# One core, LSH attention into a mixture of experts: the bucket projection reads the q and k that the scores already hold, loads move behind the exchange, v gets a third buffer, and routing and scatters move to earlier places

## The chip, the cores and the metric

The kernel runs on one core of one Trainium2 chip. The metric is the device time of one execution in microseconds (us), less is better. The engines are TensorE (PE; its weight loads are listed apart as PEld), VectorE (DVE), ScalarE (ACT), GpSimd (POOL) and SyncE (SP), which here only issues transfers. Each engine works through its own instructions in order and waits on semaphores for the others.

## The reference

Attention in which a query sees only the keys of its own bucket, then a mixture of experts with one expert per token, all in float32:

```python
q, k, v: [4, 8, 768, 64];  proj: [64, 6]
q_bits = (einsum('bhsd,dk->bhsk', q, proj) > 0)      # and the same for k
q_bucket = sum(q_bits * 2**arange(6))                # and the same for k
mask = q_bucket[:, :, :, None] == k_bucket[:, :, None, :]
scores = where(mask, (q @ k.T) / 8, -1e9)
attn = exp(scores - max);  attn = attn / (attn.sum(-1) + 1e-9)
x = (attn @ v) as [3072, 512]                        # token, 8 heads x 64
logits = x @ w_gate                                  # [512, 8]
e = argmax(logits);  gate = softmax(logits)[e]
y = gate * (relu(x @ w1[e]) @ w2[e])                 # w1 [8,512,1024], w2 [8,1024,512]
```

## The kernel before, in words

The 32 heads are worked through two at a time. I call the two heads of one step a **pair**; there are 16, numbered 0 to 15, four per batch. The outer loop is `for g in range(NG)`. What every engine does inside a pair, and in which order, is a table of words written out by hand: `HEAD` for pair 0, `NEXT` for pair 1, `PLAN` for pairs 2 to 14, `LAST` for pair 15. `step` turns a word into instructions; a word with a `-` belongs to the pair before.

The words that matter here:

- `S0` to `S11` (`score`, L302 and L304): the 12 score tiles of a pair, 128 queries by 768 keys, for its two heads in turn. The scores land in three PSUM buffers named `s`.
- `R` (`peak`, L312): VectorE's row maximum of a tile. `A` (`factor`, L317 to L321): bias and scale from it, on GpSimd where the word ends in P. `X` (`expo`, L328): ScalarE's exponential, which frees the PSUM buffer.
- `T`, `E`: half of the probability tiles are transposed on TensorE (L342) and copied out. `D` (`turn`, L382): the other half is transposed in 32x32 blocks by VectorE into the tile `w2`, and `Y` (`exchange`, L391) moves the blocks to their partitions by 16 transfers SBUF to SBUF into `pt`. It is issued at the start of the next pair.
- `B` and `V` (`pv`, L402): probabilities times v (tile `vt`). `K`, `L` (`tok`, L421, and `tok_ev`, L431): the result per token, with the gate's logits beside it.
- `G` (`lsh_mm`, L260): the projection of q and k of the next pair on the six random directions. `H` (`lsh_ev`, L243): the signs, on ScalarE. `w` (`lsh_bits`): GpSimd scales half of them and SP writes them to DRAM (`masks<-bits`, L271). `z0`, `z1` (`mask`, L275): GpSimd issues two transfers that read them back, one per head, into 16 rows of the next pair's operands (`qk` or `w`). With these rows the score product itself puts the masked scores out of reach, so `S0` and `S1` of the next pair cannot start before `z0` and `z1` have landed.
- `Z` (`route_step`): the routing of a batch (argmax of the logits, a running count per expert, the slot of each token), once per batch, in pairs 5, 9 and 13. `N` (`scatter_step`): the scatter of 128 token rows to their slots in DRAM (L496), issued by GpSimd.
- `C` (`part`): GpSimd splits the next pair's q and k into high and low parts.

The loads are called from `before(c)` when `score` starts an even tile: `load_x` (q and k of one head, `xd`, or `w` for odd pairs, 768 KB), `load_pair` (the same q and k of two heads once more, packed on 128 partitions, `xhe`, 768 KB, read by `lsh_mm` alone), `load_v` (`vt`, 384 KB) and `fill` (`sorted_rows<-xr`, 1156 KB of empty rows into the slots, eight times in all). All of them, the exchange and the write of the bits go through SP's one queue in the order of the program: what waits there holds up what stands behind it.

After pair 15 the eight experts follow, as matrix products over sorted tokens. The change leaves them as they are.

## Time and profile before

| what | value |
|---|---|
| median of 3 runs | 798.16 us (795.27 to 802.81) |
| the profiled execution | 803.59 us, of which 801.8 us lie between its first and last instruction |
| attention, pairs 1 to 14 | 35.1 to 446.5 us of the span |
| TensorE busy | 739.3 us (92%) |
| GpSimd busy | 513.0 us (64%) |
| data moved | 148.13 MB, mean 185 GB/s |

The experts fill the span's last 320 us with TensorE nearly always busy; what there is of idle time on TensorE lies in the attention. A pair is measured here from its first row maximum on VectorE (L312) to the next pair's. All times of the trace are microseconds from the first instruction of that one execution.

### The profile page before, as it was taken

Reading aid. Unit: us, or ns where it says so; the run is one execution under the profiler, and the core shown is the slowest. Engines: PE = TensorE matmul, PEld = TensorE weight load, DVE = VectorE, ACT = ScalarE, POOL = GpSimd, SP = SyncE. Lnnn points to the kernel's source line nnn. Section 1 sums busy time; section 2 is a strip of 40 time slices with the busy share of each in tenths; the row PEclk is TensorE's granted clock in tenths of the full one; section 3 lists DMA queues with packets and bytes.
Section 4 is the critical chain, followed back from the end, with each engine's and each line's share of the span. In section 5 each row is a group of like instructions: output and inputs, shape, how many; then the busy total and the mean of one; then the engine's idle time right before and its main releaser. Section 6 shows DMA issues by size and latency. Waiting matters only on the chain.

```text
span 801.8 us, 12935 instructions
## 1 busy us (share of the span) xinstructions
PE 739.3 (92%) x4315; PEld 585.6 (73%) x4315; DVE 458.7 (57%) x861; ACT 403.7 (50%) x800; POOL 513.0 (64%) x800
## 2 busy tenths in 40 slices
PE   8987979778979898899989899999999999999996
PEld 4765657355666566567656678989999999989895
DVE  7666868476758777788867856322272723232221
ACT  6765666363656565577646662443444443434320
POOL 6845757465857676787868555566465757667532
PEclk8998999899989999999988999999999999999999
DMA  7549699797896869779765843845435458545301
GB/s 262 193 153 227 192 267 250 217 248 228 236 250 155 230 172 225 225 217 247 189 178 146 212 138 138 282 131 200 165 129 183 128 147 173 164 144 190 115 9 36
DMA packets 59124, 148.13 MB, mean 185 GB/s; under 512 B 12451, under 2 KB 16291, under 8 KB 59056
## 3 DMA queue, kind: packets, MB, share of 16 engines
q1 hardware_dynamic: 52224, 130.92, 57.3%
q0 software_dynamic: 6688, 16.35, 6.2%
q8 instruction: 35, 0.57, 0.3%
q14 instruction: 33, 0.27, 0.1%
q10 hardware_dynamic: 144, 0.02, 0.0%
HBM read 88.39 MB, written 26.33 MB: 143 GB/s over the span
## 4 chain that ended last, share of the span: by engine, by line
PE 62%; DMA 14%; POOL 6%; issue 6%; DVE 5%; ACT 3%; SPq 3%; POOLq 0%; another core or an unknown queue 0%; DVEq 0%; ACTq 0%
PE s L746 16%; PE s L783 9%; PE t L402 9%; PE s L803 7%; PE s L302 6%; PE s L304 5%; PE t L342 4%; DMA qk<-masks 4%; DMA pt<-w 3%; DMA w<-masks 3%; DVE m L312 3%; PE t L421 2%; ACT e L328 2%; SPq L391 2%; DMA masks<-bits 2%
## 5 line engine op out<-in xcount | busy, mean ns | idle before, releaser
L328 ACT ACTIVATE e<-s,m 128x768 f32<-128x768 f32 x192 | 190.1, 991 | 141.4 <-POOL m L321 122.3
L312 DVE TENSOR_REDUCE m<-s 128x1 f32<-128x768 f32 x192 | 180.1, 950 | 61.6 <-PE s L304 54.2
L674 POOL TENSOR_TENSOR w<-raw,w 128x512 fp32r<-128x512 f32 x112 | 142.4, 1302 | 45.7 <-ACT w L673 45.5
L402 PE MATMUL t<-pt,vt 128*64 128x384 f32 x768 | 135.8, 504 | 16.8 <-DMA pt<-w 10.8
L746 PE MATMUL s<-xh,w 128*128 128x456 f32 (+6 forms) x672 | 126.8, 346 | 0.0
L746 PEld LDWEIGHTS s<-xh,w 128*128 128x128 f32 x672 | 119.1, 188 | 2.9
L402 PEld LDWEIGHTS t<-pt,vt 128*64 128x64 f32 x768 | 54.4, 141 | 83.9 <-issue 76.5
L342 PE MATMUL t<-ident,e 128*128 128x128 f32 x648 | 92.8, 279 | 11.2 <-ACT pt L368 7.8
L342 PEld LDWEIGHTS t<-ident,e 128*128 128x128 f32 x648 | 74.3, 141 | 26.9 <-ACT pt L368 13.1
L382 DVE STREAM_TRANSPOSE w<-e 128x768 f32<-128x768 f32 x84 | 78.5, 959 | 23.4 <-DMA pt<-w 9.1
L762 DVE SCALAR_TENSOR_TENSOR hh<-s,hh 128x256 fp32r<-128x256 f32 (+7 forms) x64 | 35.5, 555 | 91.4 <-ACT hh L760 90.0
L783 PE MATMUL s<-hh,w 128*128 128x456 f32 (+3 forms) x384 | 78.7, 359 | 0.0
L317 POOL TENSOR_SCALAR m<-m 128x1 f32<-128x1 f32 x126 | 29.4, 233 | 74.2 <-DVE m L312 70.2
L302 PE MATMUL s<-qk 80*128 80x384 f32 x192 | 60.7, 401 | 12.7 <-DMA qk<-masks 12.5
L783 PEld LDWEIGHTS s<-hh,w 128*128 128x128 f32 x384 | 69.9, 188 | 2.4
L368 ACT ACTIVATE pt<-t 128x512 f32<-128x512 f32 (+1 forms) x113 | 65.2, 588 | 12.3 <-PE t L342 11.8
L302 PE MATMUL s<-w 80*128 80x384 f32 x192 | 58.7, 387 | 13.1 <-DMA w<-masks 9.6
L760 ACT ACTIVATE hh<-s 128x256 fp32r<-128x256 f32 (+7 forms) x64 | 31.3, 489 | 75.9 <-PE s L746 75.9
L816 POOL DMA_INDIRECT out_dram<-y,ix x26 | 26.0, 999 | 67.6 <-DVE y L814 31.7
L673 ACT ACTIVATE w<-raw 128x512 fp32r<-128x512 f32 x112 | 66.4, 623 | 2.5 <-DMA raw<-in_w_dram 2.4
L803 PE MATMUL s<-w,hh 128*128 128x512 f32 (+1 forms) x240 | 58.9, 398 | 0.0
L304 PE MATMUL s<-qk 128*128 128x384 f32 x192 | 53.8, 363 | 0.7 <-DVE qk L228 0.7
(209 smaller groups left out, 1076.7 us busy)
## 6 DMA issues: line engine op xcount, KB each, us to landing
raw<-in_w_dram SPq DMA_DIRECT2D x64, 512.0 KB, 3.7
pt<-w SPq DMA_DIRECT2D x224, 144.0 KB, 4.3
xd<-in_qk_dram SPq DMA_DIRECT2D x16, 768.0 KB, 5.5
xhe<-in_qk_dram SPq DMA_DIRECT2D x15, 768.0 KB, 7.1
w<-in_qk_dram SPq DMA_DIRECT2D x14, 768.0 KB, 5.7
sorted_rows<-xr SPq DMA_DIRECT2D x8, 1156.0 KB
xg<-sorted_rows SPq DMA_DIRECT2D x25, 289.0 KB, 4.9
vt<-in_v_dram SPq DMA_DIRECT2D x16, 384.0 KB, 3.5
```

Of the source, the lines that this page charges most:

```text
L302: nc.tensor.matmul(p[:, a, :HALF], k[0:80, 2, c], k[0:80, 3, n], start=i >= 4, stop=i < 4)
L304: nc.tensor.matmul(p[:, a, :HALF], k[:, 0, c], k[:, 1, n], start=i < 4, stop=i >= 4)
L312: nc.vector.tensor_reduce(m[:, 0:1], p[:, :, :HALF], axis=AX.XY, op=OP.max, negate=True)
L328: nc.scalar.activation(e, p[:, :, :HALF], AF.Exp, bias=m[:, 2:3], scale=m[:, 1:2], accum_out=SM[g, hf][:, t, s:s + 1])
L342: nc.tensor.transpose(p[:, x * 128:(x + 1) * 128], e[w][:, kt // 3, (kt % 3) * 128:(kt % 3) * 128 + 128], ident)
L382: nc.vector.transpose(d.rearrange("p b k q -> p k b q"), PP.pop(i).rearrange("p a c -> p (a c)"))
L402: nc.tensor.matmul(p[s * 64:(s + 1) * 64, :HALF], VT[g][:, kt, s, :], x, start=(kt == 0), stop=(kt == NT - 1))
L673: nc.scalar.activation(w[:, 0, a], r, AF.Copy)
L674: nc.gpsimd.tensor_tensor(w[:, 1, a], r, w[:, 0, a], op=OP.subtract)
L746: nc.tensor.matmul(p[:, :c], w[:, a, d, fs], x[:, b, d, :c], start=(k == 0), stop=(k == 11))
L783: nc.tensor.matmul(p[:, :c], w[:, a, f % 4, ms], h[b][:, f, :c], start=(k == 0), stop=(k == 23))
L803: nc.tensor.matmul(p[:pw], HH[n][b][:, f, i:i + pw], w[:, a, f % 4], start=(k == 0), stop=(k == 23))
```

## The change

It has five parts. (1) `lsh_mm` no longer reads `xhe` but the tiles `xd` that the scores use. Those hold each head's q and k twice, on partitions 0 to 63 and 64 to 127, so the projection is now 16 products instead of 4: 64 rows deep, 192 columns wide, two heads (`s`) added up in PSUM, the two halves of the columns (`r`) on the two halves of the rows, into two PSUM buffers `t` instead of one. `lsh_ev` takes two sign instructions of 192 columns instead of one of 384. `load_pair` and its 15 loads go. (2) `load_x` of both heads moves from the words `S0` and `S4` to `S6`, so behind the exchange in SP's queue. (3) `vt` has three buffers instead of two. (4) The fills move from pairs 1 to 4 to pairs 0 to 3. (5) In `PLAN` the routing words `Z` move to the front of the pair, and the six scatters of a batch are spread: in batches 0 and 1 two in each of three pairs (words `N3` and `N4`, then `N0` and `N3` twice), where it was one, three and two; in batch 2 two and four, where it was one and five. `N4` stands between `z0` and `z1`; it was used in the first and the second of these pairs (5 and 6, 9 and 10, 13 and 14), and is now used in the first alone.

```diff
@@ -51,7 +51,7 @@
 
 
 @with_exitstack
-def lsh_attention_moe(ctx, tc, qk, qk2, v, proj, wg, w1, w2, out):
+def lsh_attention_moe(ctx, tc, qk2, v, proj, wg, w1, w2, out):
     nc = tc.nc
     const = ctx.enter_context(tc.tile_pool(name="const", bufs=1))
     moe = ctx.enter_context(tc.tile_pool(name="moe", bufs=1))
@@ -64,7 +64,7 @@
     tabd = nc.dram_tensor("spill_rows", [TMAX, 128, 2], I32).ap()
 
 
-    XD, XL, VT = {}, {}, {}
+    XD, VT = {}, {}
 
 
     room = moe.tile([128, 2, 2 * S], F32, name="w3")
@@ -76,17 +76,12 @@
             nc.sync.dma_start(x[:, c[0]:c[1]], qk2[h][:, c[0]:c[1]])
         XD[h] = x
 
-    def load_pair(g):
-        x = moe.tile([128, 2 * S], F32, name="xhe")
-        nc.sync.dma_start(x, qk[2 * g:2 * g + 2].rearrange("s d c -> (s d) c"))
-        XL[g] = x
-
     def load_v(g):
-        VT[g] = wk.tile([128, NT, 2, D], F32, name="vt")
+        VT[g] = wk.tile([128, NT, 2, D], F32, name="vt", bufs=3)
         nc.sync.dma_start(VT[g], v[g])
 
     load_x(0)
-    pj = const.tile([128, 32], F32, name="pj")
+    pj = const.tile([128, 64], F32, name="pj")
     nc.scalar.dma_start(pj, proj)
     load_x(1)
     small = const.tile([128, 1], F32, name="small")
@@ -235,7 +230,7 @@
 
         p = LP[-h, k] = ps.tile([128, 512], F32, name="t", bufs=2)
         for a in (2 * k, 2 * k + 1):
-            nc.tensor.matmul(p[32 * a:32 * a + 32, :HALF], pj[0:64], XD[h][0:64, a * HALF:(a + 1) * HALF],
+            nc.tensor.matmul(p[32 * a:32 * a + 32, :HALF], pj[0:64, 0:32], XD[h][0:64, a * HALF:(a + 1) * HALF],
                              start=True, stop=True)
 
     def signs(o, i, at=0):
@@ -254,15 +249,21 @@
 
     def lsh_mm(g):
 
-        x = XL.pop(g)
-        p = ps.tile([128, 512], F32, name="t", bufs=2)
-        for a in range(4):
-            nc.tensor.matmul(p[32 * a:32 * a + 32, :HALF], pj, x[:, a * HALF:(a + 1) * HALF], start=True, stop=True)
-        LP[g] = p
+        LP[g] = p = [ps.tile([128, 512], F32, name="t", bufs=2) for _ in range(2)]
+        n = HALF // 2
+        for s in range(2):
+            for a in range(4):
+                for r in range(2):
+                    d = slice(64 * r, 64 * r + 64)
+                    nc.tensor.matmul(p[r][32 * a:32 * a + 32, :n], pj[d, 32 * s:32 * s + 32],
+                                     XD[2 * g + s][d, a * HALF + r * n:a * HALF + r * n + n],
+                                     start=(s == 0), stop=(s == 1))
 
     def lsh_ev(g):
         BT[g] = wk.tile([128, HALF], F32, name="bits", bufs=1)
-        signs(BT[g], LP.pop(g)[:, :HALF])
+        n = HALF // 2
+        for r, p in enumerate(LP.pop(g)):
+            signs(BT[g][:, r * n:r * n + n], p[:, :n])
 
     def lsh_bits(g):
 
@@ -846,7 +847,6 @@
 
 
     late_consts()
-    load_pair(1)
     load_x(2)
     load_x(3)
     load_v(0)
@@ -890,7 +890,7 @@
 
     HEAD = """
         k01A k00V j00V j01P y01 q00A p00V y00 q01P l00V b03 p01P f0 b00 b02 l01P b01 k10A f1 k11A y11 j10P p10A R0
-        q10A S1 j11P b12 y10 R1 l10P b13 S2 X0 G b10 p11P s01 R2 X1 b11 S3 q11P H S4 X2 w R3 T00 T01 E00a l11P S5 R4
+        q10A S1 j11P b12 y10 R1 l10P b13 S2 X0 b10 p11P s01 R2 X1 b11 G S3 q11P H S4 X2 w R3 T00 T01 E00a l11P S5 R4
         E01a T02 X3 s00 R5 E02a s02 T10 X4 S6 E10v X5 R6 T11 S7 s10 E11a T12 s13 R7 E12a T20 X6 S8 s03 E20v T21 X7
         S9 z0 E21v T22 s11 R8 T30 E22a S10 s14 E30a s15 T31 X8 R9 V0 M0 X9 E31v R10 s12 z1 s05 T32 O0 s04 S11 E32a
         T40 X10 R11 K0
@@ -904,10 +904,10 @@
     """.split()
 
     PLAN = """
-        O0- S0 S1 Y0- C00 C01 C02 K0- S2 R0 R1 A0P A1P L0- G C03 C04 R2 X0 Z0 A2V S3 R3 Z1 X1 N0 S4 H A3P X2 R4 T00
-        E00a T01 S5 N1 X3 Z2 E01v T02 T10 R5 S6 A4P C05 E02v A5P R6 X4 E10a T11 X5 T12 A6V w M1- E11a S7 N2 C06 C10 S8
-        C11 R7 X6 A7V T20 E12a S9 E20v N3 R8 C12 T21 X7 R9 A8P C13 E21a C14 A9P T22 X8 z0 S10 D6 B10- E22a Z3 Z4 R10
-        Z5 Z6 D7 X9 A10P X10 N4 S11 R11 B11- B00 z1 D8 O1- A11P B01 D9 X11 C15 K1- D10 C16 D11 M0 L1-
+        O0- S0 S1 Y0- C00 C01 C02 K0- Z0 S2 R0 R1 Z1 A0P A1P L0- G C03 C04 R2 X0 Z2 A2V S3 R3 X1 N0 S4 H Z3 A3P X2 Z4
+        R4 Z5 T00 E00a T01 S5 N1 X3 E01v T02 T10 R5 Z6 S6 A4P C05 E02v A5P R6 X4 E10a T11 X5 T12 A6V w M1- E11a S7 N2
+        C06 C10 S8 C11 R7 X6 A7V T20 E12a S9 E20v N3 R8 C12 T21 X7 R9 A8P C13 E21a C14 A9P T22 X8 z0 S10 D6 B10- E22a
+        R10 D7 X9 A10P X10 N4 S11 R11 B11- B00 z1 D8 O1- A11P B01 D9 X11 C15 K1- D10 C16 D11 M0 L1-
     """.split()
 
     LAST = """
@@ -932,21 +932,21 @@
 
         b, q = divmod(g - NP, NP)
         if 0 <= b < B - 1:
-            at = {(1, 4): 0, (2, 0): 1, (2, 1): 2, (2, 2): 3, (2, 3): 4, (2, 4): 5} if b == B - 2 else                 {(1, 4): 0, (2, 0): 1, (2, 2): 2, (2, 4): 3, (3, 0): 4, (3, 2): 5}
+            late = {(2, 1): 3, (2, 2): 4, (2, 3): 5} if b == B - 2 else {(2, 3): 3, (3, 0): 4, (3, 3): 5}
+            at = {(1, 3): 0, (1, 4): 1, (2, 0): 2} | late
             if (q, k) in at:
                 scatter(b, at[q, k] // 3, (at[q, k] % 3,))
 
     def before(c):
 
         g, r = divmod(c, 6)
-        if g + 2 < NG and r in (0, 2) and g + 2 != NG - 1:
-            load_x(2 * g + 4 + r // 2)
+        if r == 3 and g + 2 < NG - 1:
+            load_x(2 * g + 4)
+            load_x(2 * g + 5)
         if g + 1 < NG and r == 4:
             load_v(g + 1)
-        if g + 2 < NG and r == 3:
-            load_pair(g + 2)
-        if 0 < g < 5 and r > 3:
-            fill((g - 1) * 2 + r - 4)
+        if g < 4 and r > 3:
+            fill(2 * g + r - 4)
 
     def behind(i):
 
@@ -1169,13 +1169,13 @@
     q, k, v = (np.asarray(inputs[n]) for n in "qkv")
     qk = np.ascontiguousarray(np.stack([q, k], 2).transpose(0, 1, 4, 2, 3)).reshape(B * H, D, 2 * S)
     vv = np.ascontiguousarray(v.reshape(B, NP, 2, NT, 128, D).transpose(0, 1, 4, 3, 2, 5)).reshape(NG, 128, NT, 2, D)
-    pj = np.zeros((2, D, 32), np.float32)
+    pj = np.zeros((2, D, 64), np.float32)
     wg = np.zeros((2, D, NP, 2 * E), np.float32)
     for s in range(2):
-        pj[s, :, s * 16:s * 16 + 12] = np.tile(inputs["proj"], 2)
+        pj[:, :, s * 48:s * 48 + 12] = np.tile(inputs["proj"], 2)
         wg[s, :, :, s * E:s * E + E] = np.asarray(inputs["moe_w_gate"]).reshape(NP, 2, D, E)[:, s].transpose(1, 0, 2)
-    pj, wg = pj.reshape(2 * D, 32), wg.reshape(2 * D, NP, 2 * E)
-    arrays = {"in_qk_dram": qk, "in_qk2_dram": np.concatenate([qk, qk], 1), "in_v_dram": vv, "in_proj_dram": pj, "in_wg_dram": wg,
+    pj, wg = pj.reshape(2 * D, 64), wg.reshape(2 * D, NP, 2 * E)
+    arrays = {"in_qk2_dram": np.concatenate([qk, qk], 1), "in_v_dram": vv, "in_proj_dram": pj, "in_wg_dram": wg,
               "in_w1_dram": np.ascontiguousarray(inputs["moe_w1"]), "in_w2_dram": np.ascontiguousarray(inputs["moe_w2"])}
     nc = bacc.Bacc("TRN2", target_bir_lowering=False, num_devices=1, dynamic_dma_scratch_size=2048)
     args = [nc.dram_tensor(n, a.shape, mybir.dt.from_np(a.dtype), kind="ExternalInput").ap() for n, a in arrays.items()]
```

SP's queue around the pairs 3 and 4, where the fills are still going. The names: `masks<-bits` is the write of the bits, `sorted_rows<-xr` two fills, `pt<-w_...` the 16 transfers of one exchange. Before:

```order
L271 DMA masks<-bits 128x384
L86 DMA vt<-in_v_dram 128x768
L149 DMA sorted_rows<-xr 512x1x578 x2
L76 DMA xd<-in_qk_dram 128x1536
L391 DMA pt<-w_1295 32x1152 x16
L76 DMA xd<-in_qk_dram 128x1536
L81 DMA xhe<-in_qk_dram 128x1536
L271 DMA masks<-bits 128x384
```

And after:

```order
L272 DMA masks<-bits 128x384
L81 DMA vt<-in_v_dram 128x768
L144 DMA sorted_rows<-xr 512x1x578 x2
L392 DMA pt<-w_1343 32x1152 x16
L76 DMA xd<-in_qk_dram 128x1536 x2
L272 DMA masks<-bits 128x384
```

The load of q and k ahead of the exchange has gone behind it, in the place of `xhe`; two loads of 768 KB still stand ahead of the write of the bits.

VectorE at the start of pair 5, where batch 0 is routed: `xr<-t,r` is the word `L`, `m<-s` a row maximum, `rl<-xr` and `rf<-rl` are the routing's reductions. Before:

```order
L431 TENSOR_TENSOR xr<-t,r 128x3x144
L312 TENSOR_REDUCE m<-s 128x1 x2
L431 TENSOR_TENSOR xr<-t,r 128x3x144
L312 TENSOR_REDUCE m<-s 128x1
L453 TENSOR_REDUCE rl<-xr 128x24 x2
L454 TENSOR_REDUCE rf<-rl 128x6
```

And after:

```order
L432 TENSOR_TENSOR xr<-t,r 128x3x144
L454 TENSOR_REDUCE rl<-xr 128x24 x2
L455 TENSOR_REDUCE rf<-rl 128x6
L313 TENSOR_REDUCE m<-s 128x1 x2
L460 TENSOR_REDUCE rf<-rl 128x6
L432 TENSOR_TENSOR xr<-t,r 128x3x144
```

The first reductions of the routing now stand ahead of the pair's first two row maxima, and its next one ahead of the `xr<-t,r` for which the projection waits.

## Rows read from the trace of the kernel before

**Rows 1.** SP's own waits, whole run: who for whom, us in total, times, longest

```profile
SPq L86 <- PE t L402: 120.3, 13, 10.5
```

**Rows 2.** Busy us (count) by engine in stretches; then granted clock, DMA share, GB/s

```profile
252.60:277.10 24.50, 24.08 (x152) 16.49 (x151) 20.97 (x34) 16.64 (x33) 18.15 (x35) 1.00 0.85 225
388.10:414.10 26.00, 24.88 (x159) 16.68 (x158) 22.44 (x43) 17.04 (x34) 18.83 (x40) 1.00 0.66 179
277.10:307.00 29.90, 26.46 (x159) 18.62 (x159) 22.74 (x43) 17.27 (x34) 20.67 (x44) 0.94 0.69 188
128.10:161.00 32.90, 26.62 (x154) 17.95 (x153) 20.93 (x34) 16.75 (x33) 18.36 (x35) 0.90 0.86 238
35.10:446.50 411.40, 361.60 (x2165) 250.50 (x2164) 298.88 (x501) 239.46 (x471) 283.07 (x547) 0.95 0.78 214
```

**Rows 3.** Waits of the engines, whole run: us in total, times, longest

```profile
PE s L302 <- DMA qk<-masks: 12.5, 4, 5.3
...
PE t L402 <- DMA pt<-w: 10.8, 3, 5.2
...
PE s L302 <- DMA w<-masks: 9.6, 3, 4.8
...
PE t L402 <- DMA xd<-in_qk_dram: 5.9, 1, 5.9
```

**Rows 4.** Timeline of TensorE: first instruction after four of these waits

```profile
69.39 0.98 PE L302 MATMUL s<-qk 80*128 80x384 f32 x2 [5.34 <-DMA qk<-masks]
...
147.88 0.91 PE L402 MATMUL t<-pt,vt 128*64 128x384 f32 x2 [5.91 <-DMA xd<-in_qk_dram]
...
279.19 0.91 PE L302 MATMUL s<-w 80*128 80x384 f32 x2 [2.14 <-DMA w<-masks]
...
461.95 1.51 PE L402 MATMUL t<-pt,vt 128*64 128x384 f32 x8 [1.39 <-DMA pt<-w]
```

**Rows 5.** Timeline of SP's issues, pairs 1, 4 and 8: start, us, what

```profile
53.03 1.31 SPq L149 DMA_DIRECT2D sorted_rows<-xr  x2
...
122.98 1.29 SPq L149 DMA_DIRECT2D sorted_rows<-xr  x2
...
125.96 17.41 SPq L391 DMA_DIRECT2D pt<-w  x16
...
263.60 0.38 SPq L271 DMA_DIRECT2D masks<-bits  x1
271.58 0.33 SPq L86 DMA_DIRECT2D vt<-in_v_dram  x1
272.00 0.38 SPq L76 DMA_DIRECT2D w<-in_qk_dram  x1
275.58 10.78 SPq L391 DMA_DIRECT2D pt<-w  x16
```

**Rows 6.** Mask reads issued at 60.30, 270.94 and 272.01: KB, us to landing

```profile
qk<-masks POOLq DMA_DIRECT2D x1, 96.0 KB, 9.0
...
w<-masks POOLq DMA_DIRECT2D x1, 96.0 KB, 2.7
...
w<-masks POOLq DMA_DIRECT2D x1, 96.0 KB, 7.0
```

**Rows 7.** Groups by line and form: busy us, mean ns of one, idle before

```profile
L260 PE MATMUL t<-xhe,pj 128*32 128x384 f32 x120 | 14.8, 568 | 0.0
...
L243 ACT ACTIVATE bits<-t,small 128x384 f32<-128x384 f32 x15 | 8.6, 576 | 6.3 <-PE t L260 6.3
...
L453 DVE TENSOR_REDUCE rl<-xr 128x24 f32<-128x192 f32 x8 | 3.9, 510 | 0.1
```

**Rows 8.** The routing's tile `rl`: ns min/median/max of one instruction on GpSimd

```profile
L461 POOL TENSOR_SCALAR oh<-rl x3: 326/326/329, 167.1 to 394.2; 128x48 bf16<-128x48 f32 x3
```

**Rows 9.** Timeline of ScalarE and TensorE at the start of pair 13

```profile
389.77 0.99 ACT L328 ACTIVATE e<-s,m 128x768 f32<-128x768 f32 x1 [2.79 <-POOL m L321]
...
390.15 0.85 PE L260 MATMUL t<-xhe,pj 128*32 128x384 f32 x8
390.94 0.62 PE L302 MATMUL s<-w 80*128 80x384 f32 x2
```

## What I predict

> **What bounds the kernel now.** I read the stretches first. Pair 8 takes 24.5 us, and TensorE is busy for 24.08 of them at a granted clock of 1.00 [rows 2]: an undisturbed pair is bound by TensorE, and the others hide behind it. Pairs 1 to 14 together take 411.4 us with TensorE busy for 361.6 and a mean clock of 0.95, so about 50 us are idle, and pairs such as 4 (32.9 us, clock 0.90) and 9 (29.9 us, clock 0.94) are well above 24.5 [rows 2]. The waits say for what: seven for a mask (12.5 and 9.6 us), three for the exchange (10.8), and one of 5.9 put down to a load of q and k [rows 3]. The timeline shows this last one at a product with v, whose other operand comes by the exchange [rows 4]; I count it with the exchange. That is 38.8 us in eleven waits, and each is a transfer that landed late.
>
> Why they land late is in SP's queue and in the landings. The load of v cannot be issued before the second product with v of the pair before has read its buffer; SP stood for this 120.3 us in all [rows 1]. It is let go at the pair's end, at 271.58 in pair 8, with the load of q and k right behind it at 272.00 [rows 5]. The first mask read went out at 270.94, ahead of both, and landed in 2.7 us; the second at 272.01, behind them, took 7.0 [rows 6], and TensorE stood for 2.14 us at its first use [rows 4]. So a read on GpSimd's queue does not overtake what SP's queue holds. For the fills it is the same: in pair 1 two were issued at 53.03 [rows 5], and the mask read of 60.30 took 9.0 us [rows 6] and cost 5.34 [rows 4]. In pairs 2 to 4 the fills wait behind the load of v until the pair's end, and stand, with a load of q and k, right ahead of the exchange: 122.98, then 125.96 with 17.41 us for the 16 issues, where those at the start of pair 9 took 10.78 [rows 5]. That is the wait of 5.91 at 147.88 [rows 4], and two more like it.
>
> **What goes.** With three buffers the load of v needs a product that ended a whole pair earlier, so it follows the write of the bits at once, some 8 us ahead of the mask reads (in pair 8 the write is at 263.60 [rows 5]). The load of q and k stands behind the exchange, in the slot of the packed copy that goes; both had the same size, so the write of the bits keeps what it has ahead of it. From pair 5 on nothing of SP is then issued right ahead of the mask reads, and the exchange, at 275.58, comes after them. I take off all 38.8 us but the exchange wait of the last pair, 1.39 at 461.95 [rows 4], where the queue stays as it was: 37.4. After each wait TensorE runs for a while at the lower of its two clock levels (1.2 and 2.4 GHz); 0.05 of 411.4 us [rows 2] is 20.6 us of full clock that was not granted, of which I take a little over half as lost on work, 12 (the rest fell into the idle time itself). Together 49. The lengths agree: pair 9 is 5.4 us over pair 8 for a wait of 2.14, pair 4 is 8.4 over for one of 5.91.
>
> **What is put in its place.** *Fills.* They are now issued behind the write of the bits in pairs 0 to 3, where those of pair 1 stood already. So the exchange is free of them, but the mask reads of pairs 1, 2 and 3 find them ahead. In pair 1 the 5.34 us had a load of q and k in the queue too, which is gone; I take 2 us each, and 1.3 for the clock: 10 us. Bounds: nothing, if the bits are ready early, and three times 5.34 with 2.5 of clock, 23. Pair 0 has until pair 1 to read its masks; I take nothing there, 3 at most.
>
> *Routing early.* In pairs 5, 9 and 13 two reductions of 0.51 us [rows 7] and a small one stand ahead of the first row maximum. Then GpSimd does five operations of about 0.33 [rows 8] ahead of the first factor, which the first exponential waits for (389.77 in pair 13); TensorE began the fourth score tile at 390.94 [rows 9], as soon as that exponential freed a buffer. The first exponential moves back by 1.0 at least and by 2.8 if all of it queues up. Pair 13 pays for the old place too: it takes 26.0 us against 24.5 for pair 8 [rows 2]. Net 1.5 a pair, so 4.5 us; bounds 0 and 8.
>
> *The projection.* Eight passes take 0.85 us on TensorE [rows 9], though one takes 568 ns on average [rows 7]: the four column quarters run side by side. Now 32 passes of half the width run on eight tiles of the array. If the two row halves also overlap, the streaming time is what it was, plus a start for twice as many rounds; if they don't, it doubles, 0.85 more. No row of this trace shows two row halves at once, and a gain has no source, since no fewer columns are streamed. I take 0.2, nearer to the overlap that the quarters show. The second sign instruction costs at most half of the 576 ns [rows 7] again, on ScalarE, which stands between two exponentials there; I take 0.1 of it as seen. So 0.3 for 15 pairs, 4.5 us; bounds 0 and 15 times 1.1, 17. The second PSUM buffer is the one that `xr<-t,r` frees; the projection waited for that before, so this is free, except in the routing pairs, where it is counted above.
>
> The page TensorEngine Tiling of the Trainium skill (Tiling Modes) lists eight tiles of 64 rows by 32 columns and says that tiles work independently; by that the term is the low one, and no run here shows it yet.
>
> *Costless.* Dropping 15 loads of 768 KB removes 11.8 of 148 MB, but TensorE waited for none of them. Two scatters fewer stand between the two mask reads (pairs 6 and 10). Elsewhere GpSimd does the same work at another place, and is busy for 18 to 21 us of the pairs shown [rows 2]: covered as long as a pair takes 24.5.
>
> **The sum.** 49 − 10 − 4.5 − 4.5 = 30 us off the profiled execution's 803.6, giving 773.6. That execution is 5.4 above the median of 798.2, so I move the result by as much: 768.
>
> **Rivals.** *The fills eat more.* All upper bounds of fills (23 and pair 0's 3) and routing at once: 49 − 26 − 8 − 4.5 = 10.5, or 788. For it speaks the wait of pair 1; against it that one load fewer is in the way.
>
> *The mask reads do not depend on SP's loads.* Then the scatter or the write of the bits delays them, and six mask waits (22.1 − 5.3 = 16.8 us) stay with half of the clock's 12. The gain is 49 − 22.8 − 9 = 17, or 781. Against it speak 2.7 and 7.0 us within 1.1 us of each other, with no scatter near [rows 6].
>
> The page DMA: Bandwidth & Descriptors of the Trainium skill (Queues, rings and completion order) says that each DMA engine takes turns between the queues that have work. By that a small read on GpSimd's queue would pass a long queue of SP's, and this rival would hold; the 7.0 us speak against it.
>
> *Slower: the projection's passes do not overlap.* If the small tiles run one after the other, 32 passes at half of 568 ns [rows 7] are 9 us instead of 0.85, all on TensorE, the engine that bounds a pair. Even 5 us a pair make 15 × 4.2 = 63, so about 798 − 30 + 59 = 827. It decides from (30 + 4.5) / 15 = 2.3 us a pair on. The four quarters that do overlap speak against it.
>
> *No change.* The waits move to other transfers, for instance a write of the bits that lands late because both loads stand before it, and the time stays near 798. Pair 8, at 24.5 with the same two loads ahead, speaks against it.
>
> **Chances.** The forecast 0.62, fills 0.13, independent reads 0.09, no change 0.09, slow projection 0.07. The range has to hold the first three, so it reaches from 748 (no fill waits, no cost of projection and routing: 798 − 49, and one more) to 789. Within 1% of 798, which is about what a measurement can tell from no change, ends at 790: faster 0.83, same 0.10, slower 0.07.
>
> **What would show it.** In the profile after: no wait of TensorE for masks from pair 5 on and mask reads of about 3 us there; exchange waits gone, with 16 issues in 10 to 12 us in every pair; small mask waits at the starts of pairs 2, 3 and 4; pairs 6, 7, 10 and 11 near 25 us; the projection under 1.1 us in a pair. It is wrong if mask waits stay in late pairs, if the fill pairs lose more than 3 us each, or if the projection takes over 2 us.

## The result, and the profile after

| | before | after |
|---|---|---|
| median | 800.1 us (795.27 to 802.81, 4 runs) | 772.43 us (768.97 to 775.15, 4 runs) |
| profiled execution, and its span | 803.59, 801.8 | 770.12, 768.1 |
| attention, pairs 1 to 14 | 411.4 us, TensorE busy 361.6 | 378.8 us, TensorE busy 353.5 |
| data moved | 148.13 MB | 136.39 MB |

The ratio is 0.9658, 95% interval 0.9587 to 0.9729: faster by 3.4%. The forecast was 768 in 748 to 789. The medians differ by 27.7 us and the profiled executions by 33.5, where the sum was 30. Nearly all of it lies in the attention: pairs 1 to 14 lost 32.6 us.

The waits of the whole run after the change (us in total, times, longest) answer to [rows 3]. Behind the "..." stand other waits, those of the experts and those for exponentials and copies among them, which were there before as well:

```profile
POOL qk L276 <- DMA masks<-bits: 9.4, 2, 5.1
...
PEld t L422 <- ACT ot L408: 4.2, 3, 2.3
...
PE t L258 <- DVE xr L432: 4.1, 6, 0.9
...
PE s L303 <- DMA w<-masks: 3.0, 1, 3.0
POOL w L276 <- DMA masks<-bits: 2.9, 1, 2.9
...
PE s L303 <- DMA qk<-masks: 0.5, 1, 0.5
```

Of 38.8 us in eleven waits for masks and exchange, 3.5 in two are left. The exchange has no row at all. What is new on TensorE is the projection's wait for its second PSUM buffer (L258) and a wait for a copy of ScalarE (`ot`). GpSimd waits 12.3 us in three places for the write of the bits. That wait is not new: before, it was 24.2 us in five places, three of them of about 7 us in pairs 3 to 5, which [rows 3] doesn't show:

```profile
POOL qk L275 <- DMA masks<-bits: 14.0, 2, 7.1
...
POOL w L275 <- DMA masks<-bits: 10.2, 3, 7.6
```

SP no longer stands at the load of v [rows 1]; it stands at the exchange, for its data, which is what it should be waiting for:

```profile
SPq L392 <- DVE r L412: 140.3, 13, 12.7
```

The stretches (busy us and count by engine, granted clock, DMA share, GB/s) of pairs 1 to 14, of pair 2, of pairs 4 and 5 and of pair 8 answer to [rows 2]:

```profile
35.70:414.50 378.80, 353.48 (x2501) 249.02 (x2500) 297.23 (x502) 240.43 (x485) 284.96 (x549) 0.98 0.73 201
66.70:95.30 28.60, 25.30 (x178) 18.12 (x177) 20.79 (x34) 16.85 (x34) 19.55 (x37) 0.96 0.97 267
121.65:173.80 52.15, 49.60 (x361) 34.78 (x360) 43.21 (x76) 34.16 (x69) 40.31 (x80) 1.00 0.69 188
225.80:251.40 25.60, 24.61 (x179) 17.42 (x178) 21.75 (x38) 16.85 (x34) 19.55 (x37) 1.00 0.73 192
```

TensorE's idle time in pairs 1 to 14 fell from 49.8 to 25.3 us, and its busy time by 8.1, with the mean clock up from 0.95 to 0.98. The waits for masks and exchange fell by 33.9 us in these pairs (the 1.39 of pair 15 left out) and the idle time by 24.5 only: some 9 us came back in other waits, 4.1 for the second buffer, 2.2 for `ot` and 1.0 for a load of q and k in pair 14 among them. Three places on TensorE's timeline are worth a look; they answer to [rows 4] and [rows 9]:

```profile
93.64 0.98 PE L303 MATMUL s<-w 80*128 80x384 f32 x2 [2.98 <-DMA w<-masks]
...
226.99 0.51 PE L258 MATMUL t<-w,pj 64*32 64x192 f32 x2
228.17 0.88 PE L258 MATMUL t<-w,pj 64*32 64x192 f32 x30 [0.68 <-DVE xr L432]
```

The first is the only mask wait that counts, behind the fills of pair 2. The others are the projection: two passes, a stop of 0.68 us until VectorE has read the buffer `t`, then 30 passes in 0.88 us. SP's queue in pair 7 and GpSimd's first mask read there answer to [rows 5]:

```profile
210.61 1.02 SPq L76 DMA_DIRECT2D w<-in_qk_dram  x2
211.72 0.38 SPq L272 DMA_DIRECT2D masks<-bits  x1
212.16 0.69 SPq L81 DMA_DIRECT2D vt<-in_v_dram  x1
225.19 10.75 SPq L392 DMA_DIRECT2D pt<-w  x16
```

```profile
220.46 0.62 POOL L276 DMA_DIRECT2D qk<-masks  x1 [4.29 <-DMA masks<-bits]
```

The load of v leaves right behind the write of the bits, and the loads of q and k ahead of it. That write was issued at 211.72 and GpSimd was let go by it at 220.46, nearly 9 us later. The mask reads themselves are short now. From 90 us of the span on, answering to [rows 6]:

```profile
DMA to landing us min/median/max: 2.6/2.8/6.3
```

### The profile page after: what moved, and what is told of

It reads as the page before. It is cut to its first block, busy times and chain, and to the rows that moved or that the text cites. A ratio compares the mean times of both kernels' runs of the same rounds, so it can differ in the third digit from the quotient of the medians.

```text
span 768.1 us, 13633 instructions
## 1 busy us (share of the span) xinstructions
PE 729.5 (95%) x4675; PEld 584.0 (76%) x4675; DVE 457.8 (60%) x861; ACT 404.5 (53%) x815; POOL 513.3 (67%) x800
## 2 busy tenths in 40 slices
DMA packets 56966, 136.39 MB, mean 178 GB/s; under 512 B 12211, under 2 KB 16051, under 8 KB 56896
## 4 chain that ended last, share of the span: by engine, by line
PE 62%; POOL 7%; issue 7%; DVE 6%; ACT 6%; DMA 6%; SPq 5%; POOLq 0%; ACTq 0%; DVEq 0%; another core or an unknown queue 0%
PE s L747 17%; PE t L403 10%; PE s L784 10%; PE s L804 7%; SPq L392 5%; PE s L303 4%; PE t L343 4%; ACT e L329 4%; PE s L305 4%; DVE m L313 3%; DMA masks<-bits 3%; PE t L422 2%; PE t L709 2%; ACT pt L369 1%; DMA xd<-in_qk_dram 1%
## 5 line engine op out<-in xcount | busy, mean ns | idle before, releaser
L403 PE MATMUL t<-pt,vt 128*64 128x384 f32 x768 | 130.9, 490 | 0.0
L403 PEld LDWEIGHTS t<-pt,vt 128*64 128x64 f32 x768 | 52.3, 137 | 64.9 <-issue 63.7
L343 PEld LDWEIGHTS t<-ident,e 128*128 128x128 f32 x648 | 74.8, 142 | 25.7 <-ACT pt L369 12.8
L817 POOL DMA_INDIRECT out_dram<-y,ix x26 | 25.9, 996 | 67.6 <-DVE y L815 31.6
L303 PE MATMUL s<-qk 80*128 80x384 f32 x192 | 56.4, 376 | 1.3 <-ACT e L329 0.6
L715 DVE TENSOR_TENSOR xh<-t,xh 128x456 fp32r<-128x456 f32 (+6 forms) x28 | 16.0, 575 | 64.3 <-ACT xh L714 64.0
```

The lines of the kernel that those rows point to most:

```text
L303: nc.tensor.matmul(p[:, a, :HALF], k[0:80, 2, c], k[0:80, 3, n], start=i >= 4, stop=i < 4)
L343: nc.tensor.transpose(p[:, x * 128:(x + 1) * 128], e[w][:, kt // 3, (kt % 3) * 128:(kt % 3) * 128 + 128], ident)
L403: nc.tensor.matmul(p[s * 64:(s + 1) * 64, :HALF], VT[g][:, kt, s, :], x, start=(kt == 0), stop=(kt == NT - 1))
```

## The experiments

The ratio is always to the kernel before, run on the same chip. The theory going in: a transfer lands late by what SP's queue was given just ahead of it; the third buffer of v and the move of the loads each take something out of the way of the mask reads; and the new projection is cheap. The rivals: only one of the two moves matters, the fills or the projection eat a good part of the gain, or the queue of a transfer decides and not the load on the DMA engines.

### The third buffer of v alone

```diff
 (before)
-        VT[g] = wk.tile([128, NT, 2, D], F32, name="vt")
+        VT[g] = wk.tile([128, NT, 2, D], F32, name="vt", bufs=3)
```

> The kernel before with nothing changed but the third buffer of v. Theory A (a mask read waits for what SP's queue was given ahead of it, and it is the load of v, held until the pair's end, that lets itself and the next load of q and k go just then): the load of v goes right behind the write of the bits, the six mask waits from pair 5 on (16.8 us) go, and the fills of pairs 2 to 4 no longer stand right ahead of the exchange, so its waits (16 us with the one put down to a load of q and k) go too; with the clock and without the new projection's cost 765 to 775 us. Theory B (the reads are held by the scatter or the write of the bits, not by SP's loads): mask waits stay, and only the exchange gains, 780 to 792.

Measured: 781.54 us, 0.9796 (0.9731 to 0.9862), outside the 765 to 775 of theory A. Its mechanism holds in the late pairs: with scatters and write of the bits left as they were, the six mask waits from pair 5 on fell from 16.8 to 3.2 us, and the exchange waits from 16.7 to 1.6. But the load of v no longer holds back the fills of pairs 1 to 4, which now stand ahead of the mask reads. TensorE at the starts of pairs 2 to 5:

```profile
68.43 0.98 PE L302 MATMUL s<-qk 80*128 80x384 f32 x2 [4.29 <-DMA qk<-masks]
98.50 0.76 PE L302 MATMUL s<-w 80*128 80x384 f32 x2 [2.59 <-DMA w<-masks]
127.80 0.59 PE L302 MATMUL s<-qk 80*128 80x384 f32 x2 [3.21 <-DMA qk<-masks]
...
158.52 0.98 PE L302 MATMUL s<-w 80*128 80x384 f32 x2 [3.93 <-DMA w<-masks]
```

Fills and a load of q and k are issued together in these pairs, as in pair 1 of before. In the late pairs SP's queue shows what the buffer does. The rows of pair 8 answer to [rows 5]:

```profile
253.06 0.38 SPq L271 DMA_DIRECT2D masks<-bits  x1
253.49 0.75 SPq L86 DMA_DIRECT2D vt<-in_v_dram  x1
254.34 0.41 SPq L76 DMA_DIRECT2D w<-in_qk_dram  x1
```

The load of q and k that in before stood behind the load of v until 272.00 [rows 5] goes out with it, 6.6 us ahead of the mask read of 260.96.

### The loads behind the exchange alone

```diff
 (before)
-        if g + 2 < NG and r in (0, 2) and g + 2 != NG - 1:
-            load_x(2 * g + 4 + r // 2)
+        if r == 3 and g + 2 < NG - 1:
+            load_x(2 * g + 4)
+            load_x(2 * g + 5)
```

> The kernel before with nothing changed but the two loads of q and k, both behind the exchange, so that three loads of 768 KB stand ahead of the write of the bits. Theory A: the load of v is still held to the pair's end, now alone, so mask reads have 384 KB ahead of them instead of 1152 and take 4 to 5 us instead of 7; fills still stand ahead of the exchange in pairs 2 to 4; the write of the bits lands about 2 us later. 785 to 795 us. Theory B (the loads' place is what the change gains by): within 5 us of the changed kernel's 772.

Measured: 791.72 us, 0.9936 (0.99 to 0.9972), in the range of theory A. Less than a fifth of the gain, and the reason is a new wait. With the packed load there are now three loads ahead of the write of the bits. GpSimd and, 3 us later, TensorE in pair 6:

```profile
204.46 0.62 POOL L275 DMA_DIRECT2D w<-masks  x1 [7.19 <-DMA masks<-bits]
```

```profile
207.19 1.68 PE L421 MATMUL t<-wgt,ot 128*128 128x144 f32 x6 [3.48 <-ACT ot L407]
```

GpSimd's factors stand behind the mask read that waits; the exponential needs a factor, ScalarE's copy `ot` stands behind the exponential, and TensorE waits for `ot`. GpSimd waited 45.6 us for this write in nine places.

### Two buffers of v again

```diff
 (after)
-        VT[g] = wk.tile([128, NT, 2, D], F32, name="vt", bufs=3)
+        VT[g] = wk.tile([128, NT, 2, D], F32, name="vt")
```

> The changed kernel with two buffers of v again. Theory A: the load of v and the fills behind it are held to the pair's end again, so the exchange waits of pairs 3 to 4 come back (about 5 us and some clock each), and mask reads of pairs 5 and later find the load of v alone ahead of them, 4 to 5 us: 778 to 788. Theory B: no difference from 772.

Measured: 774.45 us, 0.9685 (0.9619 to 0.975), no difference from after that can be measured; theory A, 778 to 788, fails. SP stands 104.0 us at the load of v again, and lets it go in the middle of the mask reads. Pair 8, SP and then GpSimd:

```profile
248.94 0.33 SPq L81 DMA_DIRECT2D vt<-in_v_dram  x1
```

```profile
248.68 0.57 POOL L276 DMA_DIRECT2D w<-masks  x1 [2.63 <-DVE w L383]
249.83 0.56 POOL L276 DMA_DIRECT2D w<-masks  x1
```

The first of these reads took 4.3 us to land, against 2.7 in pair 8 of after, and yet TensorE waits for masks only 2.6 us in the whole run. So the load of v at the pair's end hardly does harm by itself here; by this run and v3_only, what hurt was the load of q and k that went out behind it. A third buffer lets that load go early, the move puts it behind the exchange: two roads to the same gain, and with the second the first isn't needed.

### The packed copy again

```diff
 (after)
+        if g + 2 < NG and r == 3:
+            load_pair(g + 2)
```

with the old `lsh_mm`, `lsh_ev` and `pj` of before, which read it.

> The changed kernel with the old projection: the packed copy of q and k is loaded again, at the same word as the other two loads, so three loads stand ahead of the write of the bits. If the new projection costs about 1.1 us a pair on TensorE (wait for its second buffer, and passes), as pairs of 25.6 us against 24.5 say: 12 to 15 us less than the changed kernel, 757 to 762, unless the third load makes the write of the bits late, which then shows as waits of GpSimd for it. If the second copy's traffic was what cost time: 775 or more.

Measured: 785.08 us, 0.9833 (0.9767 to 0.9898): 12.7 us above after, though its projection is the old, cheaper one. SP, GpSimd and TensorE in pair 7:

```profile
216.03 1.37 SPq L76 DMA_DIRECT2D w<-in_qk_dram  x2
217.49 0.39 SPq L81 DMA_DIRECT2D xhe<-in_qk_dram  x1
217.97 1.28 SPq L271 DMA_DIRECT2D masks<-bits  x1
```

```profile
228.52 0.62 POOL L275 DMA_DIRECT2D qk<-masks  x1 [6.55 <-DMA masks<-bits]
```

```profile
231.24 1.09 PE L421 MATMUL t<-wgt,ot 128*128 128x144 f32 x3 [2.90 <-ACT ot L407]
```

The third load makes the write later still, and the same chain ends on TensorE: the case that the expectation set aside with its "unless". GpSimd waits 34.4 us for the write in seven places, where it was 12.3 in three. TensorE has no wait for `xhe`. The pairs that grew by more than 2 us over after (2, 6, 7, 10 and 12) are all pairs in which GpSimd stood 4.9 us or more for the write. What the copy's traffic would cost behind the write isn't shown; no run has it there.

### The projection on one buffer

```diff
 (after)
-        LP[g] = p = [ps.tile([128, 512], F32, name="t", bufs=2) for _ in range(2)]
+        LP[g] = p = ps.tile([128, 512], F32, name="t", bufs=2)
...
-                for r in range(2):
...
+                nc.tensor.matmul(p[32 * a:32 * a + 32, :HALF], pj[0:64, 32 * s:32 * s + 32],
+                                 XD[2 * g + s][0:64, a * HALF:(a + 1) * HALF],
+                                 start=(s == 0), stop=(s == 1))
...
```

> The changed kernel with the projection in one PSUM buffer: 8 products 64 rows deep and 384 wide on half of the rows, one sign instruction. Passes: 16 of full width on four column quarters, so TensorE is busy about 0.6 us longer a pair. If the cost of the new projection is the wait for the second buffer (0.7 to 0.9 us idle a pair behind the copy of the results per token): that wait goes and the time is 768 to 773. If it is the passes or the starts of many small ones: the cost doubles, 780 or more.

Measured: 772.47 us, 0.9706 (0.9655 to 0.9756), as after. The wait for the second buffer is gone, pair 8 is 25.9 us (25.6 after): the longer passes, 1.49 us for 16 on four column quarters, cost about what the wait did.

### Half of the projection

```diff
 (after)
...
-                for r in range(2):
...
+                nc.tensor.matmul(p[32 * a:32 * a + 32, :n], pj[0:64, 32 * s:32 * s + 32],
+                                 XD[2 * g + s][0:64, a * HALF:a * HALF + n],
+                                 start=(s == 0), stop=(s == 1))
...
```

> After, with half of the projection left out (the passes of the second half of the tokens and their PSUM buffer; the signs of the first half are written twice): 16 passes on one buffer. This prices the new form. If the projection costs some 1.1 us a pair over the old one (the wait for the second buffer of 0.7 to 0.9 and longer passes), an undisturbed pair falls from 25.6 to 24.6 or so and the time to 757 to 762. If the time is set elsewhere (factors on GpSimd, the exponentials), the pairs stay near 25.5 and the time within 768 to 773.

Measured: 768.61 us, 0.9634 (0.9595 to 0.9673). Pair 8:

```profile
226.62:252.02 25.40, 25.04 (x168) 18.03 (x167) 21.95 (x37) 16.71 (x34) 18.69 (x36) 1.00 0.74 198
```

Half of the passes and the buffer's wait are gone, and the pair is 0.2 us shorter. The second answer held. At the routing pairs part of it came back at once: TensorE waits 2.4 us there for the exponential, where it was 0.97. So the wait of 0.68 that stands on the timeline of TensorE, the engine with the highest busy share, is hardly worth anything. TensorE is listed as busy for 25.04 us of this pair, against 24.61 with all the passes: its listed busy time isn't a measure of its work alone.

### The projection one tile later

```diff
 (after, PLAN)
...
-L0- G C03 C04 R2 X0 Z2 A2V S3 R3
+L0- C03 C04 R2 X0 Z2 A2V S3 G R3
...
```

> The changed kernel with the projection one score tile later in pairs 2 to 14, so that the second buffer is free when it starts. If the wait for that buffer is the cost: TensorE's idle time there goes, 0.8 us in 13 pairs, 761 to 766. If the wait only moves (the fourth score tile waits for the first exponential instead, or the signs and the bits come late): 770 to 774.

Measured: 775.59 us, 0.972 (0.9662 to 0.9778): no gain. Pair 8 is 26.2 us, and TensorE waits instead for the exponential that frees a score buffer (0.67 to 1.36 us in most pairs, 3.16 where a batch is routed).

### The old places of routing and scatters

The `PLAN` and the table of scatters of before in the kernel after.

> The changed kernel with routing and scatters at their old places. If routing early costs 1 to 2 us in pairs 5, 9 and 13 and nothing is gained by it: 768 to 771. If the scatters between the two mask reads of pairs 6 and 10 were a cause of the mask waits of their own: two waits of 2 us or more come back, 774 to 778.

Measured: 772.85 us, 0.9708 (0.9657 to 0.976), as after. Pairs 4 and 5 together, and pair 8:

```profile
126.16:176.84 50.68, 49.34 (x361) 34.91 (x360) 43.24 (x77) 34.13 (x69) 38.67 (x77) 1.00 0.68 187
230.96:255.61 24.65, 23.66 (x173) 16.47 (x172) 20.66 (x34) 16.77 (x34) 18.65 (x36) 1.00 0.73 194
```

Pairs 4 and 5 take 50.68 us against 52.15 after: early routing costs 1.5 us in batch 0. In the other two batches it is more: pairs 8 and 9 take 51.1 against 53.4, pairs 12 and 13 50.7 against 53.1. There the clock has a part. Pair 9 of after, and pair 9 here:

```profile
251.40:279.20 27.80, 25.40 (x179) 17.77 (x179) 21.71 (x41) 17.22 (x35) 22.01 (x45) 0.94 0.70 191
```

```profile
255.60:282.00 26.40, 25.39 (x186) 17.80 (x186) 22.42 (x43) 16.98 (x35) 20.82 (x44) 1.00 0.71 191
```

In after TensorE stands for 0.87 and 0.97 us at the start of each routing pair, for the second buffer and for the exponential; in pairs 9 and 13 the granted clock then fell for a while to the lower of its two levels (1.2 of 2.4 GHz), in pair 5 it did not. In all, early routing costs 6.2 us in this pair of executions. Pairs 6, 7, 10 and 11 take 27.6, 26.5, 27.3 and 27.0 (after: 25.4, 26.6, 25.4, 27.6), so the scatters' new places give 3.4 back; the two mask waits that the expectation names come back, with 0.87 and 1.50 us and not 2. The medians lie 0.4 us apart. One more reading: pair 8 is 24.65 us here and 25.60 after in part because a pair ends at the next one's first row maximum, and in pair 9 the routing's reductions now stand ahead of it. But pair 9 isn't shorter for it, so the time is lost and not only booked elsewhere.

### The fills at their old pairs

```diff
 (after)
-        if g < 4 and r > 3:
-            fill(2 * g + r - 4)
+        if 0 < g < 5 and r > 3:
+            fill((g - 1) * 2 + r - 4)
```

> The changed kernel with the fills in pairs 1 to 4 again. Each pair's mask reads then have the fills ahead of them once more in pair 4 instead of pair 0: one more mask wait of 1 to 3 us, 772 to 777, if the fills delay mask reads. 772 without a new wait, if not.

Measured: 773.02 us, 0.97 (0.9641 to 0.9758), as after. The first answer held: a mask wait of 3.58 us stands at the start of pair 3, as in after (2.98), and a new, smaller one, 1.32, at the start of pair 5, which the later fills reach. What the fills cost hardly depends on moving all of them by one pair.

### The loads behind the write of the bits

```diff
 (after)
-        if r == 3 and g + 2 < NG - 1:
+        if r == 4 and g + 2 < NG - 1:
```

> After, with the two loads of q and k issued behind the write of the bits instead of ahead of it. Theory A (a DMA of a later issue waits behind what SP's queue holds, and what GpSimd waits for at its first mask read is this write): GpSimd's waits for masks<-bits, 2.4 to 5.1 us in pairs 7, 10 and 11, fall below 1 us, the mask reads keep their 3 us since v and the two loads still go out some 8 us ahead of them, and the time is 766 to 771. Theory B (the mask reads now find two loads and v in the queue): mask waits of 1 us and more come back in TensorE, 774 to 782.

Measured: 766.72 us, 0.9624 (0.9588 to 0.9659). SP and GpSimd in pair 7, as shown of after:

```profile
208.42 0.33 SPq L272 DMA_DIRECT2D masks<-bits  x1
208.80 1.50 SPq L76 DMA_DIRECT2D w<-in_qk_dram  x2
210.34 0.43 SPq L81 DMA_DIRECT2D vt<-in_v_dram  x1
```

```profile
216.70 0.62 POOL L276 DMA_DIRECT2D qk<-masks  x1 [0.72 <-DVE w L383]
```

The landing of the write, over pairs 1 to 14, and the stretches of pairs 7 and 11:

```profile
DMA to landing us min/median/max: 1.9/2.4/3.9
```

```profile
198.96:224.03 25.07, 24.48 (x178) 17.32 (x177) 20.69 (x33) 16.88 (x34) 20.84 (x39) 1.00 0.74 209
301.29:326.33 25.04, 24.60 (x178) 17.36 (x177) 20.75 (x33) 16.87 (x34) 20.89 (x39) 1.00 0.76 213
```

The write lands in 2.4 us where GpSimd was held for nearly 9, its waits for the write are gone, and pairs 7 and 11 fall from 26.6 and 27.6 to 25.1. The median is 5.7 us under after; the slowest of its four runs took 769.47 and the fastest of after 768.97, though the two intervals of the ratio still overlap and by the ratios the gain is only 0.3%, or 2.7 us. The profiled execution is the fastest of the four, and not all that it is shorter by comes from the write: pairs 9 and 13, 1.0 to 1.3 us shorter than in after, have the same waits as there but a clock of 1.00 for 0.94, and no run shows that the write's place did this. One mask wait is left, 3.47 us at the start of pair 2, behind the fills of pair 1.

### The write of the bits on GpSimd's queue

```diff
 (after)
-        nc.sync.dma_start(md[g], r)
+        nc.gpsimd.dma_start(md[g], r)
```

> After, with the write of the bits issued on GpSimd's queue instead of SP's. Theory A (the landing of a small transfer is set by the packets that the DMA engines already hold, whichever queue it is on): the write lands about as late as before, GpSimd still waits 2 to 5 us for masks<-bits, and the time is 770 to 775. Theory B (a transfer on another queue takes turns with SP's loads): the write lands in 2 to 3 us, these waits go, and the time is 764 to 769.

Measured: 770.8 us, 0.9653 (0.9623 to 0.9682), as after. SP's loads in pairs 7 and 8, and the landing of the two writes there, which GpSimd issued at 212.64 and 238.06:

```profile
211.36 2.35 SPq L76 DMA_DIRECT2D w<-in_qk_dram  x2
...
236.84 1.01 SPq L76 DMA_DIRECT2D xd<-in_qk_dram  x2
```

```profile
DMA to landing us min/median/max: 5.2/5.9/6.7
```

In pair 8 both loads left some 1 us ahead of the write, and it took 6.7 us. In pair 7 the second load left at 213.33, behind the write, which took 5.2. In pairs 3 and 12, both loads ahead again, the write took 6.8 us each. So 6.7 to 6.8 us stand against the 2.4 with nothing ahead. On SP's own queue behind two such loads the write took 7.2 and 6.9 us in pairs 3 and 4 of before, and nearly 9 in pair 7 of after, where the load of v follows it. The first of these, the write issued at 112.72:

```profile
DMA to landing us min/median/max: 7.2/7.2/7.2
```

Theory A held for the landing and for the time: another queue lets the write past little or nothing that is ahead of it, and how much of the 2 us against after comes from the queue isn't shown. The page DMA: Bandwidth & Descriptors of the Trainium skill (Queues, rings and completion order) says that each DMA engine takes turns between the queues that have work. The 6.7 us, beside 6.9 and 7.2, show no free pass by that.

GpSimd's waits for the write, which theory A kept, are gone: it reaches its mask reads 7 to 9 us behind the write, when that has landed. But GpSimd is busy for 296.0 us in pairs 1 to 14 against 285.0, of which the 14 issues of 0.65 us make 9.1. Whether that ate the gain wasn't tried.

### No fills in pair 1

```diff
 (loads_last)
-        if g < 4 and r > 3:
-            fill(2 * g + r - 4)
+        if g in (0, 2, 3, 4) and r > 3:
+            fill(2 * (g - (g > 0)) + r - 4)
```

> After, with the loads of q and k behind the write of the bits, as in loads_last, and the fills in pairs 0, 2, 3 and 4 instead of 0 to 3. It prices the fills, and would be the fastest version. Theory A (fills cost only where the mask reads behind them are needed soon, which is in pair 1, the one with an order of its own, and pairs 2 and 3 of loads_last at 25.2 and 25.5 us paid nothing): the mask wait of 3.47 us at the start of pair 2 goes, pair 1 falls from 34.7 to 31 us, no other wait for a mask of over 1 us appears, and the time is 761 to 765. Theory B (fills cost wherever they stand, and pairs 2 and 3 only had slack from the late start): the wait moves to pairs 3 or 5, and the time stays at 765 to 769.

Measured: 764.34 us, 0.9593 (0.9551 to 0.9634), the lowest median of all; its interval overlaps that of loads_last. Pairs 1 to 14, and pair 2, in the profiled execution, the fastest of the six:

```profile
35.79:403.93 368.14, 349.52 (x2501) 245.22 (x2500) 297.08 (x501) 240.88 (x485) 285.85 (x549) 1.00 0.74 207
...
66.55:91.38 24.83, 24.39 (x177) 17.04 (x176) 20.80 (x35) 16.82 (x34) 19.86 (x37) 1.00 0.93 263
```

The wait of 3.47 is gone and pair 1 takes 30.8 us instead of 34.7. TensorE waits for masks 0.4 us in the whole run, and pairs 2 to 4 are at 24.8, 25.3 and 25.7 though fills are issued in each. Pair 5, behind the last fills, takes 27.8 us against 26.6 in loads_last, but at a clock of 0.94 against 1.00 and with no wait for a mask; whether the fills have a part in that isn't shown. By the medians the gain is 2.4 us, less than the 3.9 of pair 1. A mask read behind fills still takes up to 7.9 us; in these pairs that is early enough.

## Why the prediction was right, and where its terms were not

The forecast, 768 in 748 to 789, holds 772.43, and its mechanism holds: mask reads and exchange were late by what SP's queue was given just ahead of them. Its terms against what the runs showed:

| term | predicted | shown | by |
|---|---|---|---|
| eleven waits and clock | −49 | waits 38.8 to 3.5; ungranted clock 20.6 to 7.6 | after |
| fills | +10 (0 to 23) | about 3.9 for pair 1, by the medians 2.4 | no_fills_in_pair_1 |
| routing early | +4.5 (0 to 8) | 1.5, 2.3 and 2.4 in the three batches, 3.4 of it given back by the scatters; median unchanged | old_routing |
| projection | +4.5 (0 to 17) | 0.15 a pair | old_routing |
| write of the bits late | not in the sum | 5.7 by the medians, 2.7 by the ratios | loads_last |

The ungranted clock is worked out as in the prediction, 0.05 of 411.4 before and 0.02 of 378.8 after. With the terms as shown the sum would be 49 − 3.9 − 6.2 − 2 − 5.7 = 31, where the profiled execution lost 33.5. The terms come from different runs, the gain of the scatters is not in it, and a difference of a few us between two of the medians is not told apart from none, so the agreement is no proof of each. The fills were put some 6 us too high and the late write 3 to 6 us too low, at nothing; that the two nearly cancel, and the forecast comes so close, is luck.

**Fills: the right place, too large.** It charged three pairs 2 us each and 1.3 for the clock. One wait of weight is left in after, 2.98 us in pair 2, which takes 28.6 us against 24.8 without it. The rival in which the fills eat more falls.

**The third buffer: a step that failed.** The prediction let the mask reads be freed by v being loaded early. v2_again has v let go between the two mask reads and pays nothing, and v3_only gets the same freedom because the load of q and k goes out with v. The load to move was that of q and k. This didn't change the sum, since the change does both.

**"TensorE waited for none of them": a step that failed.** Dropping the packed copy was put at nothing, though the prediction itself gives the copy's slot to the load of q and k. packed_again is 12.7 us slower than after: the copy stands ahead of the write of the bits. That is also why moving the loads alone gave only 5.5 us against the before of its own chip. The move puts one more load ahead of the write, and dropping the copy takes one away; only the two together pay.

**The write of the bits: a term left out.** The rival of no change named it, a write that lands late because both loads stand before it, and was set aside by pair 8 at 24.5 us with two loads ahead. That pair was one where the write was early enough; the same trace has GpSimd waiting 24.2 us for it elsewhere. In after GpSimd waits 12.3 us for it, and loads_last gets 2.7 to 5.7 us back.

**Mask reads that do not depend on SP's loads.** This rival, 781, falls with v3_only: scatters and write of the bits stayed as they were, and the late mask waits went from 16.8 to 3.2 us. With scatters and routing back at their old places, 0.87 and 1.50 us of such waits return (old_routing), so the scatter between the two reads may have had a share.

**The projection: small as predicted, for a wrong reason.** The second buffer was called free because the projection waited for `xr<-t,r` before. It did not: its passes have no idle time of TensorE ahead of them in the whole run of before [rows 7], and after the change they wait 0.68 us in pair 8. Its price is small all the same: with the old routing the pair takes 24.65 us against 24.50 [rows 2]; half of the projection gives 0.2 us back, and one buffer or a later place nothing. That the row halves overlap is shown: 30 passes end within 0.88 us, where one takes 323 ns (median), and one_buffer, with the same columns on one row half, needs 1.49 us. The page TensorEngine Tiling (Array Packing) of the Trainium skill (Tiling Modes) agrees: tiles work independently. The slow rival, 827, falls.

**The signs it named.** Right: no wait of TensorE for masks from pair 5 on; mask reads of about 3 us (median 2.8); no exchange waits, with 16 issues in 10.75 us (pair 8). Half right: pairs 6 and 10 are 25.4 us, but 7 and 11 take 26.6 and 27.6, for the late write; and of the three early mask waits one is 2.98 us, one 0.48, and one didn't come. Wrong: the projection takes 0.51 and 0.88 us of passes, not under 1.1, and 2.06 us with the wait between them, which is past the 2 us that the prediction named as a sign against itself. Yet a pair costs hardly more for it.

**Open.** Why a wait of 0.68 us on the engine that was taken to bound the pair costs next to nothing is shown only in part: in half_projection a part comes back as waits for the exponential, which suggests, and doesn't show, that TensorE and the chain from row maximum to exponential bound a pair together. Why the clock fell in pairs 9 and 13 of after and not in pair 5, behind the same waits, stays open too. And whether other fills than those of pair 1 still cost anything wasn't tried; no run goes without them.

## What to carry to other kernels

Look at what a queue was given in the few microseconds ahead of a small transfer that someone waits for, and not only at the transfers that are waited for: here the kernel took 12.7 us more with a load there that TensorE never waits for. Put the small, urgent transfer first and the bulk loads right behind it, so that they have landed before the next urgent one; here that one line took the median from 772.4 to 766.7 and the waits for the write to nothing. And before a wait on the busiest engine is charged, see whether taking it away shortens the period: here three experiments took away a wait of 0.7 us, and pair 8 got 0.2 us shorter in one, 0.3 and 0.6 longer in the others.

## What the runs showed of the hardware

A transfer of 192 KB landed in 2.4 us (median) with nothing just ahead of it (loads_last). Behind two loads of 768 KB issued some 1 us earlier on SP's queue it took 6.9 and 7.2 us on the same queue (before, pairs 4 and 3), and 6.7 to 6.8 us on GpSimd's queue (write_on_gpsimd, pairs 3, 8 and 12): the other queue was hardly a way past them. In after, with a load of 384 KB right behind it, GpSimd was let go by it nearly 9 us after its issue (pair 7).

A load of 384 KB issued between two reads of 96 KB (v2_again, pair 8) made the first land in 4.3 us instead of 2.7, and cost TensorE nothing there.

Thirty fp32 passes of 64 rows by 32 columns, 192 wide, on both row halves ended within 0.88 us. The sixteen passes of one_buffer, 384 wide and on one row half, took 1.49.
